# Forward stage of an adaLN transformer kernel: column turns of K, Q and LayerNorm rows moved from TensorE to DMA transposes, and the filler work redistributed over four segments

## The chip, the cores and the metric

One Trainium2 chip, one of its cores. The metric is the device time of one execution in microseconds, as the median of several runs. The profile is that of one execution, with the times of every instruction and DMA issue. Engines: PE is TensorE, PEld its weight loads, DVE is VectorE, ACT is ScalarE, POOL is GpSimd, SP is SyncE. SP does nothing in this kernel but issue DMAs, in program order.

## The reference

The reference runs an adaLN block forward and backward: `_out, _vjp = jax.vjp(_f, ...)`, and returns the output and eleven gradients. What matters here is the forward recurrence, over 64 segments of 32 tokens (model width 512, 32 heads of 128, 8 memory rows, 2048 tokens):

```python
for s in range(n_seg):
    xs = x[:, s * seg_len:(s + 1) * seg_len, :].copy()
    h = jnp.concatenate([mem, xs], axis=1)
    q = jnp.einsum('btd,dhe->bhte', h, Wq)
    k = jnp.einsum('btd,dhe->bhte', h, Wk)
    v = jnp.einsum('btd,dhe->bhte', h, Wv)
    scores = jnp.einsum('bhqe,bhke->bhqk', q, k) * scale
    scores = jnp.where(mask[None, None], scores, -1000000000.0)
    p = _softmax(scores, axis=-1)
    o = jnp.einsum('bhqk,bhke->bhqe', p, v)
    o = jnp.einsum('bhte,hed->btd', o, Wo)
    mem = o[:, :M, :].copy()
    outs.append(o[:, M:, :])
```

Ahead of it stands `h = _layernorm(x) * (1 + ca) + sa`; behind it a second LayerNorm and a gated MLP, and then the whole backward pass. Each segment's first 8 rows (its memory) come from the segment before, so the 64 segments are a chain.

## The kernel before, in words

The kernel is one program in stages. `phase2` is the forward recurrence and the only stage that the change touches; the later stages (MLP forward and backward, the attention's backward recurrence, weight gradients) are the same.

In `phase2` one pass of the loop `for s in range(NS)` handles one segment. Four segments are a **tile** of 128 rows; `s4 = s % 4`. A segment has 40 rows, of which 32 (memory and the first 24 tokens) depend on the chain or are handled with it. The last 8 token rows of each segment, its **tail**, do not depend on memory in their K, Q and V rows. They are therefore computed for a whole tile at once, ahead of time, as PE filler.

Order of one segment on PE: K and Q products of 32 rows (L257), V products (L659), turn of K and Q rows into columns on PE (`turns`, L829), scores (L839), Exp on ACT into `ET` (L841), denominators (L845), P·V (L865), scaling into `Ost` on DVE and ACT (L886, L889), turn of `Ost` into `OT` (`ott`, L857), output product (`outproj`, L223), split into two bfloat16 parts (`split_pair`, L230 and L232), their fold (`sum_pair`, L242), and the copy of the new memory into `hT_next` (L1022), with which the next segment begins. Mask products (`mask_mm`, L783) open the score banks of the next segment.

Into this chain the kernel puts independent work, at named places:

- `fill(s4, "f1")` stands behind the output product, `fill(s4, "f2")` behind the fold, `fill(s4, "turn")` behind the last P·V product. `b_pieces(t)` says what goes there: the tail rows of K and Q of the *next* tile, 8 blocks of 128 columns each (`proj_b`, a call of `col_pass`, L257), written to `RB["k"]` and `RB["q"]`, stored to DRAM by `rows_out` (six DMAs each, L599 and L602) and turned into columns by `turn_b` (L623): eight PE transposes into PSUM, then copies by ACT and DVE into `b_colsk`, `b_colsq`. `tails_in` (POOL, L65) copies each segment's part of these columns into the K and Q operands.
- `p1(j, k)` runs step k of the first LayerNorm of tile j, two tiles ahead: 0 load, 1 statistics, 2 scale, 3 shift, 4 turn (four PE transposes, L420, an ACT copy into `hx`, L422, and a POOL copy of its tail columns into `hb`, L424).
- `TailRows` (object `tail`) does the output product of the four tails of the *previous* tile: 32 accumulating steps (L215), here in pieces of (24, 8) in segment 3, then a split (L314, L315), a fold (L325) and row stores, put into the list `later` and taken from it by `pop_later`.

The order on every engine is that of the program: `self.pin(i0)` ties each instruction to the one before it on its engine. SP's order in one segment is: VT store (L1040), PS store (L1041, of the segment before, after POOL has normalised `Pst`, L1038), K row stores (L594, L595), Q row stores, the transpose of `Vst` into `VTr` (L954), the transpose of `ET` into `Pst` (L962), stores OSR (L997) and OT (L1010), and then, where they fall, the tail row stores (L599, L602), a load of `wmod_r` (L195) and one of x (L394). `Pst`, `VTr`, `ET`, `Ost` and `OT` have one buffer each, so that a later write waits for the DMA that reads it. DMAs of SP use eight semaphores in turn: each waits for the landing of the eighth before it.

Of the kernel before, what the change touches and what calls it, by code (L numbers as in the profile page):

```python
# [9 lines left out]
AF = mybir.ActivationFunctionType  # L10
# [30 lines left out]
class K:  # L41
# [334 lines left out]
    def phase1_setup(self, ctx, psum_tile_fn):  # L376
        nc, tc, cfg, io = self.nc, self.tc, self.cfg, self.io
        D, DC, NT = cfg.D, cfg.DC, cfg.NT
        x_rows = io["A_x"].rearrange("o s d -> (o s) d")
        p1 = ctx.enter_context(tc.tile_pool(name="p1", bufs=1))  # L380
        p1w = ctx.enter_context(tc.tile_pool(name="p1w", bufs=2))
        ca1_bc = self.ca1_bc = p1.tile([128, D], F32, name="ca1_bc")
        sa_bc = self.sa_bc = p1.tile([128, D], F32, name="sa_bc")
        mhalf = p1.tile([128, 1], F32, name="mhalf1")
        nc.gpsimd.memset(mhalf[:], -0.5)
        nseg = 128 // cfg.T

        def p1_tile(j):

            st = {}  # L390

            def load():
                st["x0"] = p1w.tile([128, D], BF16, name="x0_1", bufs=1)
                nc.sync.dma_start(st["x0"][:], x_rows[j * 128:(j + 1) * 128, :])  # L394

            def stats():
                bs = p1w.tile([128, 6], F32, name="st1")
                nc.vector.bn_stats(bs[:], st["x0"][:])
                mv = p1w.tile([128, 2], F32, name="mv1")
                nc.vector.bn_aggr(mv[:], bs[:])  # L400
                ve = p1w.tile([128, 1], F32, name="ve1")
                nc.vector.tensor_scalar_add(ve[:], mv[:, 1:2], EPS)
                rstd = p1w.tile([128, 1], F32, name="rstd1")
                nc.gpsimd.tensor_tensor(rstd[:], ve[:], mhalf[:], op=ALU.pow)
                st.update(mv=mv, rstd=rstd)

            def scale():
                xh = st["xh"] = p1w.tile([128, D], F32, name="xh", bufs=1)
                nc.vector.tensor_scalar(xh[:], st["x0"][:], st["mv"][:, 0:1], st["rstd"][:, 0:1], op0=ALU.subtract, op1=ALU.mult)
                nc.vector.tensor_tensor(xh[:], xh[:], ca1_bc[:], op=ALU.mult)  # L410

            def shift():
                h1 = st["h1"] = p1w.tile([128, D], BF16, name="h1", bufs=1)
                nc.vector.tensor_tensor(h1[:], st["xh"][:], sa_bc[:], op=ALU.add)
                nc.gpsimd.dma_start(self.H1ROWS[j * 128:(j + 1) * 128, :], h1[:])

            def turn():
                tp = psum_tile_fn()
                for c in range(DC):
                    nc.tensor.transpose(tp[:, c, :], st["h1"][:, c * 128:(c + 1) * 128], self.ident[:])  # L420
                hx = p1w.tile([128, DC, 128], BF16, name="hx", bufs=3)
                nc.scalar.activation(hx[:], tp[:, 0:DC, :], AF.Copy)  # L422
                hb = p1w.tile([128, DC, nseg, 8], BF16, name="hb", bufs=2)
                nc.gpsimd.tensor_copy(hb[:], hx[:].rearrange("p c (s t) -> p c s t", t=cfg.T)[:, :, :, 24:cfg.T])  # L424
                return hx, hb

            return load, stats, scale, shift, turn

        return p1_tile

# [8 lines left out]
    def phase2(self):  # L439
        nc, tc, cfg, io = self.nc, self.tc, self.cfg, self.io  # L440
# [14 lines left out]
        with ExitStack() as ctx:  # L455
# [38 lines left out]
            P1_AHEAD = 2  # L494
            NT = cfg.NT
            nseg_t = 128 // T
            hxs = {}

            def p1(j, k=None):
                if j < NT:  # L500
                    if j not in p1s:
                        p1s[j] = p1_tile(j)
                    for i in (range(1, 5) if k is None else [k]):
                        r = p1s[j][i]()
                        if r is not None:
                            hxs[j] = r
# [101 lines left out]
            def b_pieces(t):  # L608

                bt = btails[t] = {}  # L610
                RBt = RB

                def proj_b(x, a, n, eng):
                    hb = hxs[t][1]
                    self.col_pass(psp, Ws[x], 0, lambda c: hb[:, c, :, :].rearrange("p s q -> p (s q)"), RBt[x], eng, steps=(a, n))
                    if a + n == 8:
                        rows_out(RBt[x], DR[x], t * nseg_t, nseg_t)

                def turn_b(x):
                    bt[x] = btp.tile([128, 8, 128], BF16, name="b_cols" + x)  # L620
                    tp = psp.tile([128, 8, 128], BF16, name="turn_ps", tag="p")
                    for i in range(8):
                        nc.tensor.transpose(tp[:, i, :], RBt[x][:, i * 128:(i + 1) * 128], self.ident[:, :])  # L623

                    def f():
                        for hf in range(2):
                            self.evac(("act", "dve")[hf], bt[x][:, 4 * hf:4 * hf + 4, :], tp[:, 4 * hf:4 * hf + 4, :])

                    evacs.append(f)

                P = lambda x, a, n, eng: (lambda: proj_b(x, a, n, eng))
                T_ = lambda x: (lambda: turn_b(x))
                return {(0, "f1"): [P("k", 0, 4, "dve")], (1, "f1"): [P("k", 4, 4, "dve")], (1, "f2"): [P("q", 0, 2, "act")],
                        (2, "turn"): [T_("k")], (2, "f1"): [P("q", 2, 4, "dve")], (2, "f2"): [P("q", 6, 2, "act")],
                        (3, "turn"): [T_("q")]}

            evacs = []

            def evac_turned():
                while evacs:  # L640
# [1 line left out]

            first = b_pieces(0)
            firsts = {x: [first[k][0] for k in ks] + [evac_turned]
                      for x, ks in (("k", ((0, "f1"), (1, "f1"), (2, "turn"))),
                                    ("q", ((1, "f2"), (2, "f1"), (2, "f2"), (3, "turn"))))}
            slots = {}

            VCH = ((0, 4), (4, 4), (8, 3))

# [51 lines left out]
            def fill(s4, where):  # L702
                for f in slots.pop((s4, where), []):
                    f()
# [67 lines left out]
                    nc.gpsimd.dma_start(self.AOA[4 * b + i + 1, 32:32 + M, :].rearrange("r (c x) -> (r c) x", x=128),  # L772
                                        rb[32 * i:32 * i + 32, :])

            tail = TailRows(self, sb2, psp, psp, 1, "ao", rows_b, (24, 8), ptag="p")

            masked = {}

# [24 lines left out]

            for s in range(NS):
                s4 = s % nseg_t
                if s4 == 0:
                    if s > 0:
                        p1(s // nseg_t + P1_AHEAD, 0)
                    slots = b_pieces(s // nseg_t + 1) if s + nseg_t < NS else {}
                hT = get_ht(s)  # L810
                hT_next = get_ht(s + 1) if s + 1 < NS else None
                QT, KT, Vst = XT["q"], XT["k"], Vsts[s % 2]
# [90 lines left out]

                if s < NS - 1 and norms:
                    norms.pop()()
                if s == NS - 1:
                    first_tile[3]()
                proj("k", 0, "dve")
# [21 lines left out]
                    v_tails(0)  # L930
                if s == NS - 1:
                    first_tile[4]()
                v_chunk(s, 0)
                turns()
                v_chunk(s, 1)
# [30 lines left out]
                ost(0, or0, "dve")  # L966
                ost(1, or1, "act")
                den(2, or2)
                if s4 == 3:
                    p1(s // nseg_t + P1_AHEAD, 4)  # L970
                early = s4 == 0 and len(self.later) > 1
                if early:
                    self.pop_later()
                more = list(range(NP)) if s + 1 < NS else []
                if more:
                    mask_mm(more.pop(0))
                pv(2, or2)
                recip(2, 3, or2)
                ost(2, or2, "dve")
                fill(s4, "turn")  # L980
                if s == NS - 1:
                    turn_v(2)
                if more and s4 < 2:
                    mask_mm(more.pop(0))
                ott(0)
                if more:
                    mask_mm(more.pop(0))
                ott(1)
                ott(2)
                if not early:  # L990
                    self.pop_later()
                self.pop_later()
                if s == NS - 1:
# [3 lines left out]
                nc.sync.dma_start(self.OSR[s], gl3(Ost))  # L997
                at_ps = outproj()
                evac_turned()
                if s4 < 3:  # L1000
                    p1(s // nseg_t + P1_AHEAD, s4 + 1)
                if NS - 4 <= s < NS - 1:
                    first_tile[s - NS + 4]()
                elif s == NS - 1:
# [7 lines left out]
                if s == NS - 1:  # L1012
                    first_tile[7]()
                    nc.scalar.activation(self.first_st[:, 11:12], self.first_st[:, 10:11], AF.Sigmoid)
                if s4 == 3:
                    tail.chunk()
                if s == NS - 1:
                    turn_p(0)
# [7 lines left out]
                if s + 1 in mod_at:  # L1026
                    load, products = self.mod_rest(psp, sb2, mod_at.index(s + 1))
                    load()
                    mod_r.append(products)
                if s4 == 3:  # L1030
                    tail.chunk()
                tail.split()
                self.store_rows(psp, sb2, ft, self.AOA[s + 1, 0:32, :], "at", "p")
# [1205 lines left out]
class TailRows:  # L2239
# [45 lines left out]
    def split(self):  # L2285
        if self.whole is None:
            return False
        (ps, s0), self.whole = self.whole, None
        parts = self.k.fold_split(self.pool, ps, self.name + "_b", self.home)

        def summed():
            ft = self.k.fold_sum(self.psp, parts, self.name + "_b", "p")
            to = self.dram_b
            to = (lambda rb: self.dram_b(rb, s0 // 4)) if callable(to) else to[s0 // 4]
            self.k.store_rows(self.psp, self.pool, ft, to, self.name + "_b", "p")

        self.k.later.append(summed)
        return True
# [100 lines left out]
```

## Time and profile before

| | us |
|---|---|
| median of 3 runs | 2996.63 (2991.85 to 3003.91) |
| span of the profiled execution | 2991.0 |
| first products and loads of `phase2` (segment 0) | 18.0 to 60.5 |
| segments 1 to 3 | 60.5 to 102.8 |
| tiles 1 to 14 (segments 4 to 59) | 102.8 to 904.1 |
| last tile (segments 60 to 63) | 904.1 to about 965 |
| PE busy, tiles 1 to 14 | 798.6 of 801.3 |
| mean DMA share, tiles 1 to 14 | 0.88 |

The span is counted from the first to the last instruction of the profiled execution; the runs' times include what lies around it. The profile's page gives busy time per engine, groups of instructions and DMA queues; other views of the trace give busy time in chosen stretches, an engine's instructions in order of time, and all instructions of one line or tile. A DMA issue on SP's queue (SPq) has as its time how long the queue was held by it, not how long the transfer took. The DMA share is the time of all packets over that of 16 engines, so a stretch can show over 1 when its packets end later. Matmul durations overlap; the cost of a group is read from its start to the start of the next.

### The profile page before, as it was taken

What the parts mean: (1) busy time and instruction counts of PE and PEld (TensorE: products, weight loads), DVE (VectorE), ACT (ScalarE), POOL (GpSimd) and SP (SyncE); (2) the same over time, 40 slices, a digit from 0 to 9 for tenths busy, and PEclk for the clock granted to TensorE, in tenths of its full rate; (3) what the DMA queues carried; (4) which work ended last, traced back from release to release, by engine and by line L of the source; (5) the groups of instructions that cost most, each with busy time, mean ns of one, the idle gap of its engine ahead of it and who ended that gap; (6) DMA issues with size and microseconds to landing.
All of it is one profiled execution on the core that took longest, in us unless ns stands there. A gap on an engine that the chain in (4) does not pass through costs nothing.

```text
span 2991.0 us, 105890 instructions
## 1 busy us (share of the span) xinstructions
PE 2932.8 (98%) x43975; PEld 1839.9 (62%) x44049; DVE 1612.4 (54%) x3679; ACT 1271.8 (43%) x3057; POOL 1197.2 (40%) x2456
## 2 busy tenths in 40 slices
PE   6999999999999999999999999999999999999999
PEld 3666666666665544445677777777777754445454
DVE  5566656666655788833456665566566532222230
ACT  2555555555555533312355555555555520011111
POOL 2454555555545222221344444444444422333321
PEclk8999999999999999999999999999999999999999
DMA  9898888889889899998699999999999997766574
GB/s 310 222 223 211 214 217 217 213 214 215 217 218 277 211 230 226 229 290 278 200 251 251 251 253 243 250 250 250 255 255 250 254 281 245 242 207 214 178 245 144
DMA packets 836438, 703.05 MB, mean 235 GB/s; under 512 B 536643, under 2 KB 708851, under 8 KB 835061
## 3 DMA queue, kind: packets, MB, share of 16 engines
q1 hardware_dynamic: 710756, 486.09, 65.5%
q0 software_dynamic: 54640, 148.90, 15.7%
q10 hardware_dynamic: 70560, 61.28, 6.5%
q8 instruction: 347, 5.69, 0.8%
q14 instruction: 135, 1.10, 0.1%
HBM read 294.99 MB, written 276.35 MB: 191 GB/s over the span
## 4 chain that ended last, share of the span: by engine, by line
PE 87%; issue 5%; DMA 3%; DVE 2%; POOL 1%; ACT 1%; SPq 1%; DVEq 0%; POOLq 0%; ACTq 0%
PE pass_ps L257 14%; PE gps L2180 9%; PE dh_ps L215 8%; PE pass_ps L659 5%; PE g_ps L1810 5%; PE gps5o L2195 4%; PE dhq_ps L223 4%; PE at_ps L223 4%; PE mm L1291 3%; PE dh_tps L215 3%; PE gps L1470 3%; PE turn_ps L829 2%; PE mm L1266 2%; PE mm L1251 1%; PE tps L1727 1%
## 5 line engine op out<-in xcount | busy, mean ns | idle before, releaser
L2180 PE MATMUL gps<-rows,hrows 128*128 128x512 bf16 (+2 forms) x2125 | 415.6, 355 | 1.8
L2180 PEld LDWEIGHTS <-hrows 128*128 128x128 bf16 x2160 | 211.3, 98 | 204.5
L61 ACT ACTIVATE ot<-gps 128x512 bf16<-128x512 f32 (+3 forms) x75 | 41.3, 550 | 362.2 <-PE gps L2180 229.1
L1855 POOL COPY dOst<-RAd 96x512 bf16<-96x512 bf16 x128 | 75.3, 613 | 297.8 <-DVE RAd L63 297.8
L1038 POOL TENSOR_TENSOR Pst<-Pst,rden 120x1408 bf16<-120x1408 bf16 x63 | 159.9, 2538 | 77.8 <-issue 49.6
L659 PE MATMUL pass_ps<-Wv,hT 128*32 128x512 bf16 (+2 forms) x2304 | 187.2, 358 | 0.0
L63 DVE CAST ot<-gps 128x512 bf16<-128x512 f32 (+3 forms) x76 | 48.1, 633 | 247.0 <-PE gps L2180 169.9
L2184 POOL DMA_DIRECT2D out_dram<-ot x108 | 81.5, 755 | 249.1 <-DVE ot L63 141.9
L257 PEld LDWEIGHTS <-hT 128*32 128x32 bf16 x4096 | 114.8, 97 | 103.9 <-issue 5.7
L63 DVE CAST Vst<-pass_ps 96x512 bf16<-96x512 f32 x128 | 87.3, 682 | 107.0 <-ACT RBv L61 98.5
L215 PE MATMUL dh_ps<-WvT,dVT 128*32 128x512 bf16 x2048 | 133.3, 380 | 1.7
L659 PE MATMUL pass_ps<-Wv,hb 128*32 128x512 bf16 (+2 forms) x636 | 128.7, 353 | 0.0
L257 PE MATMUL pass_ps<-Wq,hT 128*32 128x512 bf16 x2048 | 123.9, 383 | 4.8 <-DMA Wq<-in_A_Wq_dram 4.8
L257 PE MATMUL pass_ps<-Wk,hT 128*32 128x512 bf16 x2048 | 123.2, 382 | 2.5 <-POOL hT L549 1.1
L223 PE MATMUL at_ps<-Wo,OT 128*32 128x256 bf16 x4096 | 123.9, 273 | 0.7 <-DMA Wo<-in_A_Wo_dram 0.6
L257 PE MATMUL pass_ps<-WoT,dyT 128*32 128x256 bf16 (+1 forms) x3072 | 122.5, 308 | 0.9 <-ACT dyT L1936 0.9
L223 PE MATMUL dhq_ps<-WqT,dQT 128*32 128x256 bf16 x4096 | 122.9, 273 | 0.0
L215 PE MATMUL dh_ps<-WkT,dKT 128*32 128x512 bf16 x2048 | 122.3, 380 | 0.0
L794 POOL DMA_DIRECT2D Vst<-RBv x192 | 99.9, 526 | 55.6 <-ACT ET L841 34.4
L2195 PE MATMUL gps5o<-WoT,rows 128*128 128x512 bf16 x548 | 120.6, 379 | 1.0 <-DMA rows<-OSR 0.4
L223 PEld LDWEIGHTS <-dQT 128*32 128x32 bf16 x4096 | 109.7, 97 | 15.8
L315 DVE TENSOR_TENSOR dST<-dh_ps,dST 128x512 bf16<-128x512 f32 x64 | 44.3, 692 | 129.9 <-ACT dST L314 129.9
(471 smaller groups left out, 6991.2 us busy)
## 6 DMA issues: line engine op xcount, KB each, us to landing
OSR<-Ost SPq DMA_DIRECT2D x64, 352.0 KB
OT<-OT SPq DMA_DIRECT2D x64, 352.0 KB
PS<-Pst SPq DMA_DIRECT2D x64, 352.0 KB
Pst_l<-PS SPq DMA_DIRECT2D x64, 352.0 KB
OT_l<-OT SPq DMA_DIRECT2D x64, 352.0 KB
DVR<-rows_x POOLq DMA_DIRECT2D x64, 352.0 KB, 6.3
DKR<-rows_x POOLq DMA_DIRECT2D x64, 352.0 KB, 5.7
DQR<-rows_x POOLq DMA_DIRECT2D x64, 352.0 KB, 3.4
```

Source lines behind the costliest of these rows:

```text
L63: return nc.vector.tensor_copy(out, in_)
L215: self.nc.tensor.matmul(ps[32 * j:32 * j + 32, :], lhsT=lhsT, rhs=w, start=(n < 4), stop=(n >= total - 4), tile_position=(0, 32 * j))
L223: nc.tensor.matmul(ps[32 * j:32 * j + 32, :], lhsT=x[k], rhs=w[k][:, 256 * d:256 * d + 256], start=(n == 0), stop=(n == total - 1), tile_p ...
L257: self.nc.tensor.matmul(ps[32 * j:32 * j + 32, :], lhsT=lhs(c), rhs=rhs, start=(c == 0), stop=(c == DC - 1), tile_position=(0, 32 * j))
L659: nc.tensor.matmul(ps[32 * j:32 * j + 32, o * E:(o + n) * E], lhsT=lhsT, rhs=wc[:, 3 * a + hl:3 * (a + n - 1) + hl + 1:3, :], start=(c == ...
L794: nc.gpsimd.dma_start(Vst[96 + 8 * j:104 + 8 * j, :], rb[32 * j + o:32 * j + o + 8, :])
L1038: nc.gpsimd.tensor_tensor(Pst[0:120, :, :], Pst[0:120, :, :], rden[:, :].unsqueeze(2).to_broadcast([120, G, 128]), op=ALU.mult)
L1291: nc.tensor.matmul(hp[:], lhsT=xT[:, fc, :], rhs=wT[:, fc, :], start=(n == 0), stop=(n == 2 * FC - 1))
L1470: nc.tensor.matmul(ps[:], lhsT=h2r[:, j, c * 128:(c + 1) * 128], rhs=xr[:, j, :], start=(j == 0), stop=(j == NT - 1))
L1810: nc.tensor.matmul(ps[:, j, 0:w], lhsT=lh[:, g * GW:(g + 1) * GW], rhs=rh[:, g * GW:g * GW + w], start=True, stop=True)
L2180: nc.tensor.matmul(ps[:, 0:ng * E], lhsT=hrows[:, tp_, c * 128:(c + 1) * 128], rhs=rows[:, tp_, 0:ng * E], start=(tp_ == 0), stop=(tp_ == ...
L2195: nc.tensor.matmul(pss[gg][:], lhsT=rows[:, t, gg * E:(gg + 1) * E], rhs=dyrows[:, t, :], start=(n == 0), stop=(n == NTP - 1))
```

## The change

1. For tiles after the first, `turn_b` issues one DMA transpose of `RB[x]` (128x1024) on SP instead of eight PE transposes, an ACT and a DVE copy.
2. From tile 2 on, `p1`'s turn is one DMA transpose of `h1` (128x512) on SP. The POOL copy into `hb` becomes a step of its own (5, `ends`).
3. The pieces of `b_pieces` begin one segment earlier, in segment 3 of the tile two ahead of use, and stand in other places; the turns stand at a new place, `fill(s4, "rows")`, ahead of the V products.
4. `p1`'s steps are one segment earlier, with the load issued at the start of segment 3 (by SP's order right behind the OT store of segment 2).
5. The tail product is cut into (8, 16, 8) and lies in segments 1 and 2 instead of 3; its fold comes in segment 3 instead of 0, and the DVE copy of its rows after the turns of `Ost`.
6. The three mask products stand in the same places in all segments.

```diff
             def turn():
-                tp = psum_tile_fn()
-                for c in range(DC):
-                    nc.tensor.transpose(tp[:, c, :], st["h1"][:, c * 128:(c + 1) * 128], self.ident[:])
                 hx = p1w.tile([128, DC, 128], BF16, name="hx", bufs=3)
-                nc.scalar.activation(hx[:], tp[:, 0:DC, :], AF.Copy)
+                if j < 2:
+                    tp = psum_tile_fn()
+                    for c in range(DC):
+                        nc.tensor.transpose(tp[:, c, :], st["h1"][:, c * 128:(c + 1) * 128], self.ident[:])
+                    nc.scalar.activation(hx[:], tp[:, 0:DC, :], AF.Copy)
+                else:
+                    nc.sync.dma_start(hx[:], st["h1"][:], transpose=True)
                 hb = p1w.tile([128, DC, nseg, 8], BF16, name="hb", bufs=2)
-                nc.gpsimd.tensor_copy(hb[:], hx[:]...)
+                st.update(hx=hx, hb=hb)
+                if j < 2:
+                    ends()
                 return hx, hb
+            def ends():
+                nc.gpsimd.tensor_copy(st["hb"][:], st["hx"][:]...)
...
                 def turn_b(x):
                     bt[x] = btp.tile([128, 8, 128], BF16, name="b_cols" + x)
+                    if t > 0:
+                        nc.sync.dma_start(bt[x][:], RBt[x][:, 0:1024], transpose=True)
+                        return
...
-                return {(0, "f1"): [P("k", 0, 4, "dve")], (1, "f1"): [P("k", 4, 4, "dve")], (1, "f2"): [P("q", 0, 2, "act")],
-                        (2, "turn"): [T_("k")], (2, "f1"): [P("q", 2, 4, "dve")], (2, "f2"): [P("q", 6, 2, "act")],
-                        (3, "turn"): [T_("q")]}
+                pieces = {(3, "f1"): [P("k", 0, 4, "dve")], (3, "f2"): [P("k", 4, 2, "act")], (0, "f1"): [P("q", 0, 4, "dve")],
+                          (0, "f2"): [P("k", 6, 2, "act")], (1, "rows"): [T_("k")], (1, "f1"): [P("q", 4, 4, "dve")],
+                          (2, "rows"): [T_("q")]}
+                if t == 1:
+                    pieces[0, "f1"] = pieces.pop((3, "f1")) + pieces.pop((3, "f2")) + pieces[0, "f1"]
+                return pieces
...
-            slots = {}
+            slots = b_pieces(1)
...
-            tail = TailRows(self, sb2, psp, psp, 1, "ao", rows_b, (24, 8), ptag="p")
+            tail = TailRows(self, sb2, psp, psp, 1, "ao", rows_b, (8, 16, 8), ptag="p")
...
-                if s4 == 0:
-                    if s > 0:
-                        p1(s // nseg_t + P1_AHEAD, 0)
-                    slots = b_pieces(s // nseg_t + 1) if s + nseg_t < NS else {}
+                if s4 == 3:
+                    p1(s // nseg_t + P1_AHEAD + 1, 0)
+                    slots = b_pieces(s // nseg_t + 2) if s + 2 * nseg_t < NS + 3 else {}
...
+                if s4 == 3:
+                    p1(s // nseg_t + P1_AHEAD, 5)
...
+                fill(s4, "rows")
+                if s4 == 2:
+                    p1(s // nseg_t + P1_AHEAD, 4)
                 v_chunk(s, 0)
...
-                if s4 == 3:
-                    p1(s // nseg_t + P1_AHEAD, 4)
-                early = s4 == 0 and len(self.later) > 1
+                early = s4 == 3 and len(self.later) > 1
                 if early:
-                    self.pop_later()
+                    rows_of = self.later.pop(0)(False)
...
-                fill(s4, "turn")
-                if more and s4 < 2:
+                if more:
                     mask_mm(more.pop(0))
...
-                if not early:
+                if early:
+                    rows_of()
+                else:
                     self.pop_later()
...
-                if s4 < 3:
-                    p1(s // nseg_t + P1_AHEAD, s4 + 1)
+                if s4 == 3:
+                    p1(s // nseg_t + P1_AHEAD + 1, 1)
+                elif s4 < 2:
+                    for k in (1, 2) if s == 0 else (s4 + 2,):
+                        p1(s // nseg_t + P1_AHEAD, k)
...
-                if s4 == 3:
+                if s4 == 2:
                     tail.chunk()
...
-                if s4 == 3:
+                if s4 in (1, 2):
                     tail.chunk()
```

## The prediction

> **What bounds the kernel now.** I read the page first, then the busy time of four stretches of the forward stage, then two timelines of the same stretches: TensorE's (PE) and SyncE's queue (SPq). A *segment* is one pass of the loop over `s`; four segments make a *tile* of 128 rows.
>
> ```profile
> PE 2932.8 (98%) x43975; PEld 1839.9 (62%) x44049; DVE 1612.4 (54%) x3679; ACT 1271.8 (43%) x3057; POOL 1197.2 (40%) x2456
> ```
>
> ```profile
> 732.90:747.15 14.25, 14.11 (x281) 9.50 (x278) 9.45 (x24) 8.06 (x21) 6.71 (x13) 1.00 1.05 217
> 747.15:761.17 14.02, 14.02 (x282) 8.99 (x279) 9.00 (x22) 7.73 (x21) 7.91 (x13) 1.00 0.86 202
> 761.17:775.20 14.03, 14.03 (x292) 9.52 (x285) 8.81 (x21) 8.33 (x22) 6.89 (x15) 1.00 0.92 226
> 775.20:790.05 14.85, 14.85 (x304) 10.36 (x297) 7.72 (x19) 8.99 (x24) 8.24 (x21) 1.00 0.86 219
> ```
>
> These are segments 48 to 51 (bounds: the first Wk,hT matmul of each). After the length come PE, PEld, DVE, ACT and POOL busy, then clock, DMA share, GB/s. PE is busy throughout, at full clock; a tile takes 57.15 us, and nearly every tile from segment 12 to 59 repeats these lengths. But the last columns say that the 16 DMA engines are at 0.86 to 1.05. So PE sets the end, and something else is close behind.
>
> A full PE row can still hide waits. PE in segments 49 and 50, from the last PV product to the last transposes of Ost:
>
> ```profile
> 756.18 0.37 PE L783 MATMUL st_ps<-maskT,ident 128*128 128x480 bf16 x1
> 756.52 0.39 PE L857 MATMUL tps<-ident,Ost 120*128 120x120 bf16 x4
> 756.74 0.32 PE L783 MATMUL st_ps<-maskT,ident 128*128 128x360 bf16 x1
> 756.90 0.64 PE L857 MATMUL tps<-ident,Ost 120*128 120x120 bf16 x7
> ...
> 770.20 0.61 PE L623 MATMUL turn_ps<-ident,RBk 128*128 128x128 bf16 x8
> 770.64 0.38 PE L857 MATMUL tps<-ident,Ost 120*128 120x120 bf16 x4
> 770.85 0.37 PE L783 MATMUL st_ps<-maskT,ident 128*128 128x480 bf16 x1
> 771.06 0.53 PE L857 MATMUL tps<-ident,Ost 120*128 120x120 bf16 x7
> ```
>
> Segment 49 needs 1.36 us here (756.18 to 757.54) without a turn, segment 50 needs 1.39 (770.20 to 771.59) with one. The eight transposes, 0.44 us (770.20 to 770.64), lie in a wait for DVE's Ost.
>
> Now SyncE's queue from segment 50 into 51:
>
> ```profile
> 766.22 0.36 SPq L1041 DMA_DIRECT2D PS<-Pst  x1
> 766.68 0.51 SPq L594 DMA_DIRECT2D KST<-RA0k  x1
> 767.25 1.67 SPq L595 DMA_DIRECT2D KST<-RA0k  x1
> 769.02 0.63 SPq L594 DMA_DIRECT2D QST<-RA0q  x1
> 769.70 0.42 SPq L595 DMA_DIRECT2D QST<-RA0q  x1
> 770.38 1.94 SPq L954 DMA_TRANSPOSE VTr<-Vst  x1
> 772.77 1.50 SPq L962 DMA_TRANSPOSE Pst<-ET  x1
> 774.37 0.90 SPq L997 DMA_DIRECT2D OSR<-Ost  x1
> 775.37 0.39 SPq L1010 DMA_DIRECT2D OT<-OT  x1
> 775.86 2.60 SPq L599 DMA_DIRECT2D QST<-RBq  x3
> ```
>
> Each row is one issue and how long the queue was held. There is hardly a gap. And the queue is a closed round: the PS store waits for POOL's norm of Pst (L1038, 2.54 us); the norm waits for the Pst transpose to land (issue 757.60, norm from 763.14: 5.5 us); that transpose is queued behind VTr, and VTr behind the K and Q stores, which stand behind the previous PS store. PS issues at 738.43 and 795.43 bracket a tile: 57.00 us, PE's own period. How much of it is slack shows ahead of VTr, the one place where the queue waits for PE's chain (Vst): idle beyond the 0.23 us that every such step has is 0, 0.42, 0.03 and 0 us in these segments, so the round costs 56.55 us. In segments 28 to 31 the same reckoning gives 57.0 - 1.24 - 1.43 - 0.48 - 0 = 53.8 us. **The queue has 0.6 to 3.3 us of slack per tile.** This decides the case.
>
> **The change, part by part**, per tile.
>
> *PE, removed.* Turn of K (0.44 us), of Q (0.45, 784.61 to 785.06) and of h1 (0.22, L420): 1.11 us; over 15, 15 and 14 tiles 16.5 us (the built program has 296 transposes fewer on PE and 44 more on SP, so the change does what it says). Were all of it on the path, that would be the gain.
>
> *PE, what it was worth.* Segment 2: the turn hid a wait; the mask product goes back to its place in segment 49's pattern, so 14.03 becomes 13.96 (segment 49 without the 0.06 us ao_b transpose, which moves on to segment 0). Segment 1: 13.96. Segment 3: h1's turn (0.22) goes, the tail product shrinks from 24 steps (1.40 us, 787.75 to 789.15) to a four-block pass (0.97, 759.34 to 760.31), and the fold sum (0.20) comes in but lies in the same wait for Ost: 14.85 becomes 14.2. Segment 0: the fold sum leaves and the Ost wait shrinks (the last transposes take 0.88 us in segment 48, 0.64 in 49), -0.27; the ao_b transpose +0.06; the K blocks in the second slot +0.45 beside a mod product that already covered that wait: 14.5. Sum 56.6, **-0.55 us per tile**. Pass columns are the same in number; evacuations removed (ACT 0.60 and DVE 0.42 per turn, ACT 0.6 for hx) were not on the path. Tile 0 takes ten blocks in its first slot instead of four: +1.2 us. The last segment loses its tail product: -1.5.
>
> *SP, added.* Three transposes ahead of VTr: K in segment 1; Q and hx in segment 2. Such transposes are not in this stage, so by the nearest rows: one of 128x512 (L1197, forward MLP) holds the queue 1.20 us, minimum and median; one of 128x1408 (L962) 1.29 to 3.16, median 1.83. hx is the first: 1.2 to 1.3. K and Q (1024 columns) lie between, 1.25 to 1.8; I take 1.5, interpolated by columns. With 0.06 us between issues: 1.5 + 1.5 + 1.25 + 0.2 = **4.4 us per tile**, bounds 3.8 and 5.2. A gain from them is excluded, as they release nothing that the round waits for. The RB stores move a segment earlier and the x load to the end of segment 2: the same issues, no cost; the x load (about 1 us) lies in the norm's wait.
>
> *What is queued behind.* VTr, Pst, OSR and OT, then RB rows, VT, PS. Columns are needed one to two segments later, so their own landing costs nothing. Late is Pst: the next segment's Exp writes ET, which that transpose reads. Exp starts 6.9 us into a segment (768.05 - 761.17) while Pst has landed 2 us into it (norm 763.14); about 4 to 5 us of delay are free, once. After that PE waits.
>
> *The round after.* 53.8 to 56.55, plus 4.4. I take 55.4 (the middle of the two, moved slightly to the fuller, since the queue will be full): **59.8 us per tile**, against PE's 56.6. So the queue sets the period, 2.65 us above today's 57.15.
>
> [...]
>
> **Sum.** Thirteen tiles (2 to 14) at +2.65 = 34.5; tile 0 +1.2; tile 1, still on free slack, -0.55; end -1.5: +33.6, less 0.6 for slack left in tile 2: +33 on the profiled span of 2991.0, so 3024. The runs' median lies 5.6 us above that span; I add it: **3030 us**.
>
> **Rivals.**
> - *The queue keeps pace* (chance 0.30). If the round after stays below PE's 56.6, the gain is PE's: 13 x -0.55 + 1.2 - 0.55 - 1.5 = -8, so 2983 of span and a median of 2988. For it: segments 28 to 31, where 53.8 + 3.8 = 57.6 is within 1 us of PE's period; VTr's hold also varies from 1.28 to 2.7 us, so some of it may be backpressure that the new transposes merely take over. Against: segments 48 to 51. [...]
> - *All removed PE time counts* (0.06): only if Ost's wait did not exist; 16.5 us, 2980. Segments 49 and 50 side by side speak against it.
> - *The slower side* is my forecast (0.64): the round decides once the added issues exceed the slack of 0.6 to 3.3 us. Its own range: 53.8 + 3.8 = 57.6 gives +0.45 x 13, 3001; 56.55 + 5.2 = 61.8 gives +4.6 x 13, 3056.
> - *A held PSUM bank*: the tail product now keeps its bank through all of segment 2. Segment 3 today holds it 1.9 us only; five banks serve passes that free theirs in 1 to 2 us, so I count none. If PE lost one evacuation (0.7 us) per tile: +9 us, inside the range.
>
> **Numbers.** About 0.5% (15 us) is what a measurement of this kernel can tell from no change. Faster by more: 0.06. Within: the rival at 2988 and the lower end of my own case, 0.33. Slower: 0.61. The range takes in the rival's 2988 and goes up to 3052, leaving about 0.1 on each side.
>
> **What would show it.** Right: PE idle ahead of or behind the Exp of segments 3 and 0 that the waits put to the Pst transpose; VTr issued 10 to 14 us into segments 2 and 3 instead of 9 to 10; PS to PS four segments apart near 60 us; PE no longer 98% in slices 2 to 12. K and Q transposes should hold the queue about 1.5 us, hx 1.2. Wrong: VTr back at 8.7 us in segment 0, tiles of 56.6 us. If a transpose of 1024 columns holds the queue well below 1.2 us, or VTr's hold falls by what they take, the forecast falls with it.

## The result, and the profile after

The changed kernel took 3027.82 us (median of 4 runs, 3026.20 to 3032.19), the kernel before 2998.64 beside it: ratio 1.0106, 95% interval 1.0088 to 1.0124. The profiled execution spans 3025.8 us against 2991.0, +34.8. By the first Wk,hT products of the segments, +2.7 of that arise up to segment 3, +29.5 in tiles 1 to 14 (59.34 us each instead of 57.24), +2.5 behind them.

The page's engine line, after:

```profile
PE 2942.4 (97%) x43679; PEld 1850.2 (61%) x43753; DVE 1596.8 (53%) x3649; ACT 1249.2 (41%) x3013; POOL 1191.0 (39%) x2456
```

PE has 296 matmuls fewer and is busy 9.6 us longer. Busy time in the segments of one tile, 16 to 19 (columns as in the prediction: length, five engines, clock, DMA share, GB/s):

```profile
284.54:298.83 14.29, 14.29 (x292) 9.29 (x284) 9.27 (x22) 7.90 (x22) 7.52 (x14) 1.00 0.97 216
298.83:312.94 14.11, 14.11 (x276) 9.94 (x273) 8.02 (x20) 8.04 (x22) 8.54 (x20) 1.00 0.93 212
312.94:328.02 15.08, 14.16 (x272) 8.99 (x269) 7.01 (x17) 7.46 (x20) 6.39 (x13) 1.00 0.93 208
328.02:348.89 20.87, 16.80 (x296) 11.67 (x296) 9.86 (x25) 8.22 (x22) 7.14 (x15) 0.84 0.88 200
```

Two things are new in segment 19: PE stands still for 4.1 us (20.87 - 16.80), and the granted clock is 0.84. Other tiles run clean, that is without such a wait: segments 36 to 39 take 14.29, 14.10, 13.96 and 14.43, together 56.79. The wait, first on ACT, then on PE (in brackets the idle time before the instruction and its releaser):

```profile
339.36 1.39 ACT L854 ACTIVATE ET<-st_ps 128x480 bf16<-128x480 f32 x3 [4.74 <-DMA Pst<-ET]
```

```profile
339.99 0.27 PE L858 MATMUL or_ps<-ones,ET 128*128 128x1 bf16 x4 [3.87 <-ACT ET L854]
```

Exp may not overwrite `ET` until the Pst transpose of segment 18 has read it. SyncE's queue shows why that is late:

```profile
324.88 0.35 SPq L1061 DMA_DIRECT2D PS<-Pst  x1
325.34 0.53 SPq L602 DMA_DIRECT2D KST<-RA0k  x1
325.92 1.06 SPq L603 DMA_DIRECT2D KST<-RA0k  x1
327.09 1.08 SPq L602 DMA_DIRECT2D QST<-RA0q  x1
328.22 0.42 SPq L603 DMA_DIRECT2D QST<-RA0q  x1
328.69 2.23 SPq L630 DMA_TRANSPOSE b_colsq<-RBq  x1
330.96 1.26 SPq L425 DMA_TRANSPOSE hx<-h  x1
332.45 1.27 SPq L972 DMA_TRANSPOSE VTr<-Vst  x1
333.77 1.78 SPq L980 DMA_TRANSPOSE Pst<-ET  x1
```

These issues belong to segment 18 (312.94 to 328.02; the PS store is that of 17), and its Pst transpose goes out 5.75 us into segment 19. The queue has hardly a gap; two new transposes, 3.5 us, stand ahead of VTr. Over the tiles (waits from 102 to 920 us: total, times, longest):

```profile
ACT ET L854 <- DMA Pst<-ET: 29.0, 11, 4.7
PE or_ps L858 <- ACT ET L854: 22.8, 25, 3.9
```

And the clock behind the wait, in stretches of 2 us:

```profile
338.00:340.00 2.00, 0.01 (x1) 0.02 (x2) 0.00 (x0) 0.64 (x2) 0.31 (x1) 0.86 0.71 275
342.00:344.00 2.00, 2.00 (x15) 1.52 (x14) 1.24 (x4) 0.82 (x4) 1.95 (x5) 0.50 0.47 177
348.00:350.00 2.00, 2.00 (x52) 1.33 (x52) 1.25 (x4) 0.58 (x2) 0.17 (x1) 1.00 2.12 155
```

For 6.83 us from 339.4 the clock is 0.50, and the 64 output products, 1.76 us in clean segments, take 2.6. In tiles 1 to 14 this happens six times, 30.7 us in all, and never in the kernel before. An estimate from these figures: 14 x 56.7 (clean tiles), + 22 us of added PE idle (24.9 against 3.0 before), + half of 30.7 for the slow clock = 831; measured 830.8. It comes out a little too well, since some of the slow time lies inside the waits and clean tiles go up to 57.0.

### The profile page after: what moved, and what is told of

Its sections match the earlier page's. It is cut to its first block, busy times and chain, and to the rows that moved or that the text cites. A ratio compares the mean times of both kernels' runs of the same rounds, so it can differ in the third digit from the quotient of the medians.

```text
span 3025.8 us, 105199 instructions
## 1 busy us (share of the span) xinstructions
PE 2942.4 (97%) x43679; PEld 1850.2 (61%) x43753; DVE 1596.8 (53%) x3649; ACT 1249.2 (41%) x3013; POOL 1191.0 (39%) x2456
## 4 chain that ended last, share of the span: by engine, by line
PE 59%; issue 4%; ACT 1%; POOL 1%; DMA 1%; DVE 1%; SPq 0%; POOLq 0%; DVEq 0%; ACTq 0%
PE gps L2200 9%; PE dh_ps L215 8%; PE g_ps L1830 5%; PE pass_ps L257 5%; PE gps5o L2215 4%; PE dhq_ps L223 4%; PE mm L1311 3%; PE dh_tps L215 3%; PE gps L1490 3%; PE mm L1271 2%; PE mm L1286 2%; PE tps L1747 2%; PE mm L1240 1%; PE mm L1244 1%; PE gps L1389 1%
## 5 line engine op out<-in xcount | busy, mean ns | idle before, releaser
L61 ACT ACTIVATE ot<-gps 128x512 bf16<-128x512 f32 (+3 forms) x75 | 41.2, 550 | 363.4 <-PE gps L2200 213.0
L257 PEld LDWEIGHTS <-hT 128*32 128x32 bf16 x4096 | 127.2, 97 | 96.6 <-issue 8.3
L223 PEld LDWEIGHTS <-OT 128*32 128x32 bf16 x4096 | 105.9, 99 | 16.1 <-DVE OT L63 3.4
```

Of the source, the lines that this page charges most:

```text
L223: nc.tensor.matmul(ps[32 * j:32 * j + 32, :], lhsT=x[k], rhs=w[k][:, 256 * d:256 * d + 256], start=(n == 0), stop=(n == total - 1), tile_p ...
L257: self.nc.tensor.matmul(ps[32 * j:32 * j + 32, :], lhsT=lhs(c), rhs=rhs, start=(c == 0), stop=(c == DC - 1), tile_position=(0, 32 * j))
```

## The experiments

Per tile, from the traces (means of tiles 1 to 14). "Hold" is the sum of SP's issue times; "at PS" and "at Pst" the queue's gaps ahead of these two issues; "slack" its gap ahead of VTr beyond 4 x 0.23; PE idle (the sum of its gaps) and "slow", the time at clock 0.50, are totals of the 14 tiles. Ratios are to the kernel before on the same chip. Columns from "tile" on come from the one execution that was profiled; for e2 that was the slowest of six (3016.14 us, the others from 3000.52 on), for e3 the fastest of four (3024.51, the others up to 3038.40).

| kernel | median us | ratio, 95% interval | tile | hold | at PS | at Pst | slack | PE idle | slow |
|---|---|---|---|---|---|---|---|---|---|
| before | 2998.64 | | 57.24 | 44.5 | 6.3 | 0.4 | 1.48 | 3.0 | 0 |
| after | 3027.82 | 1.0106 (1.0088 to 1.0124) | 59.34 | 49.8 | 4.8 | 0.3 | 0.02 | 24.9 | 30.7 |
| e1_turns_on_pe | 3013.98 | 1.0062 (1.0047 to 1.0077) | 58.08 | 43.8 | 5.6 | 0.4 | 3.27 | 6.9 | 0 |
| e2_ps_late | 3006.62 | 1.0037 (1.0022 to 1.0052) | 57.68 | 49.9 | 0.7 | 2.1 | 0.57 | 11.1 | 3.4 |
| e3_et2 | 3033.30 | 1.0122 (1.0103 to 1.0141) | 58.64 | 49.2 | 4.6 | 0.3 | 0.00 | 20.4 | 20.5 |
| e4_hx_on_pe | 3023.61 | 1.0090 (1.0070 to 1.0111) | 58.61 | 48.7 | 5.2 | 0.3 | 0.05 | 18.9 | 3.4 |
| f1_ps_late_qrows | 3020.17 | 1.0068 (1.0054 to 1.0083) | 58.64 | 50.8 | 0.8 | 2.5 | 0.17 | 19.4 | 6.8 |
| f2_before_ps_late | 2999.13 | 1.0005 (0.9996 to 1.0014) | 57.20 | 41.2 | 0.5 | 2.5 | 5.58 | 2.7 | 0 |
| f5_before_dma_turns | 3055.10 | 1.0189 (1.0175 to 1.0204) | 60.73 | 49.1 | 6.6 | 0.4 | 0.06 | 40.0 | 37.5 |
| g1_rows_on_pool | 3038.31 | 1.0129 (1.0116 to 1.0143) | 60.08 | 42.3 | 13.3 | 0.3 | 0.08 | 34.0 | 27.3 |
| g2_rows_pool_ps_late | 3002.94 | 1.0008 (0.9999 to 1.0017) | 56.90 | 43.2 | 3.3 | 1.5 | 2.06 | 3.3 | 0 |
| h1_turns_behind_ot | 3027.27 | 1.0097 (1.0083 to 1.0111) | 58.91 | 51.3 | 2.8 | 0.4 | 0.13 | 24.5 | 6.8 |
| h2_turns_behind_ot_ps_late | 3037.23 | 1.0120 (1.0103 to 1.0137) | 59.39 | 49.5 | 0.4 | 5.0 | 0.25 | 30.5 | 3.4 |

The stages behind the recurrence are the same program in all runs, the ladder g3 below included, yet from segment 63 on they took 2042.6 to 2055.7 us in the profiled executions, so effects are read from the tiles.

**e1: the turns back on PE, everything else as changed.**

```diff
-                if j < 2:
+                if True:
...
-                    if t > 0:
-                        nc.sync.dma_start(bt[x][:], RBt[x][:, 0:1024], transpose=True)
-                        return
...
-                          (0, "f2"): [P("k", 6, 2, "act")], (1, "rows"): [T_("k")], (1, "f1"): [P("q", 4, 4, "dve")],
-                          (2, "rows"): [T_("q")]}
+                          (0, "f2"): [P("k", 6, 2, "act")], (1, "turn"): [T_("k")], (1, "f1"): [P("q", 4, 4, "dve")],
+                          (2, "turn"): [T_("q")]}
...
-                fill(s4, "rows")
-                if s4 == 2:
-                    p1(s // nseg_t + P1_AHEAD, 4)
                 v_chunk(s, 0)
...
+                if s4 == 2:
+                    p1(s // nseg_t + P1_AHEAD, 4)
...
+                fill(s4, "turn")
```

> The changed kernel with all three turns back on TensorE, in the stretch ahead of the Ost transposes, and everything else of the change kept. Queue theory (the three transposes make SyncE's round of 59.5 us per tile longer than PE's 56.7): the round falls back to 54 to 57 us, Exp does not wait for the Pst transpose, tiles of about 57.2 us, time 2990 to 3003. Rival, the new places of the filler passes and the tail product (with its PSUM bank held through a segment) cost the time: it stays at 3020 to 3030.

Hold 43.8, slack 3.27, no Exp wait for the Pst transpose, no slow clock: the transposes are what fills the queue. The round, tile less slack, is 58.08 - 3.27 = 54.8 us here, against 57.24 - 1.48 = 55.8 in the kernel before. Segments 38 and 39:

```profile
601.16:616.21 15.05, 14.71 (x284) 9.84 (x281) 7.62 (x18) 8.44 (x22) 7.81 (x20) 1.00 0.95 220
616.21:630.53 14.32, 14.26 (x296) 10.06 (x296) 9.59 (x25) 8.23 (x22) 7.05 (x15) 1.00 0.76 191
```

Segments 0 and 3 take 14.29 and 14.32, as in the changed kernel's clean tiles. Both time ranges missed (measured 3014, between them), for a reason outside the theories: segment 2 takes 15.05 instead of 13.96. Q's and h1's turns now both fall there, and by the timeline h1's ACT copy (0.61 us) goes ahead of the evacuation of OT, with 0.31 us of PE wait ahead of the output product. So in the tiles no cost of spreading the filler shows, but PE turns at these places cost 1.4 us a tile over a clean one.

**e2: the PS store behind the next segment's K and Q row stores.**

```diff
-                if s < NS - 1 and norms:
-                    norms.pop()()
+                put_ps = norms.pop()() if s < NS - 1 and norms else None
...
                 proj("q", 1, "act")
+                if put_ps:
+                    put_ps()
```

> The changed kernel with only the PS store issued later: behind the K and Q row stores of the next segment and not ahead of them, so that the queue does not stand still while POOL normalises Pst. All transposes stay, bytes and packets are the same. Queue theory (a round closed by the norm): the stores no longer stand in the round, Exp stops waiting, tiles of 56.6 to 56.9 us, time 2986 to 2996, below the kernel before. Rival, the DMA engines themselves are full (share 0.99): nothing changes, 3018 to 3030.

Same issues, another order: the wait at PS falls from 4.8 to 0.7 us, the tile by 1.66. The gain was not all that the theory expected (57.68, not 56.9 at most; 3006.62 us, not below the kernel before), and the rival of no change missed too. Over tiles 1 to 14 the DMA share of the changed kernel was 0.92, and 0.79 to 1.13 in single segments. Many tiles are clean (segments 20 to 27: 56.7 each), the rest wait in segment 3. Part of the gain comes back as a new wait: the Pst transpose overwrites `Pst` and must let the late PS store land first (the queue's own waits):

```profile
SPq L981 <- DMA PS<-Pst: 24.4, 23, 1.8
```

**e3: two `ET` buffers** (space from other buffers: `hx` has two instead of three).

```diff
-            ET = ptiles("ET", 1)[0]
+            ETs = ptiles("ET", 2)
```

> The changed kernel with two ET buffers, so that Exp need not wait for the Pst transpose of the segment before (to make room, hx has two buffers and the scaled rows of the first LayerNorm use the scratch of the first MLP tile). Queue theory: the round of about 59.5 us per tile is as long as before, so PE is stopped a little later by the next single buffer, Ost (read by the OSR store) or OT, and the time stays at 3012 to 3028. Rival, the single ET buffer is the cause: 2986 to 2996.

The Exp wait is gone and another stands in its place, on the next buffer that the queue reads late:

```profile
DVE Ost L902 <- DMA OSR<-Ost: 21.6, 10, 3.9
ACT Ost L899 <- DMA OSR<-Ost: 21.1, 10, 3.9
```

The slack ahead of VTr is 0.00: the queue is the limit, and `ET` only where it first showed. The median, 3033.30 us, lies above the expected range; as the profiled execution was the fastest, its tiles do not show why.

**e4: h1's turn back on PE, K and Q by DMA.**

```diff
-                if j < 2:
+                if True:
...
-                if s4 == 2:
-                    p1(s // nseg_t + P1_AHEAD, 4)
                 v_chunk(s, 0)
...
+                if s4 == 2:
+                    p1(s // nseg_t + P1_AHEAD, 4)
```

> The changed kernel with the LayerNorm turn (hx) back on TensorE, in the stretch ahead of the last PV product in segment 2; K and Q stay DMA transposes. Queue theory by hold time (hx holds the queue 1.27 us of 4.5 added): the round falls by 1.3 to 1.5 us per tile, time 3006 to 3014. Rival, the cost goes by columns moved (512 of 2560): 3020 to 3024. If only redistribution counts: 3026 to 3032.

Hold falls by 1.1 only, the wait at PS rises by 0.3, segment 2 takes 14.53 us at the median instead of 13.96 (waits included), the slack stays near nothing. One transpose fewer is not enough; the expectation was too good. The time, 3023.61, lies in the range of the rival by columns moved, and nothing here tests that rival further.

**f1: e2, with Q's tail row stores moved to segment 2.**

```diff
-                    if a + n == 8:
+                    if a + n == 8 and (x == "k" or t == 0):
...
+                if t > 0:
+                    pieces[2, "f1"] = [lambda: rows_out(RBt["q"], DR["q"], t * nseg_t, nseg_t)]
```

> The kernel of e2 with the six row stores of Q's tail moved, for tiles 1 to 15, from the end of segment 1 to behind the OT store of segment 2; no issue is added or left out. Theory that the queue's order and length set the waits (it holds 49.9 us in a tile of 56.6, so it need not be the limit if no stretch of it is late): no Exp waits for the Pst transpose, tiles of 56.7 to 56.9 us, 2986 to 2996 us. Rival, that the total of the queue's holds and landings keeps it behind wherever its issues stand: tiles as in e2, 57.5 to 58, 3002 to 3010 us.

Worse than e2, and slower than both expectations. VTr's holds grew from 8.8 to 9.8 us a tile, the wait at Pst from 2.1 to 2.5, and the Exp waits, small now, fall in segments 2, 3 and 0. Here the issues moved out of one full segment filled another.

**f2: the kernel before with e2's edit alone.**

> The kernel before with only the PS store issued later, behind the next segment's K and Q row stores. Theory that PE sets the pace of the kernel before and its queue has slack: no change, tiles of 57.1 to 57.25 us, 2992 to 3002 us. Rival, that the queue holds the kernel before too (the slack ahead of VTr was nearly 0 in segments 49 to 51): faster, tiles of 56.7 or less, 2980 to 2990 us.

The slack rises from 1.48 to 5.58 us a tile and the time stays: the kernel before is bound by PE, as the prediction read it, and the late store is worth something only where the queue is full.

**f5: the kernel before with the three DMA turns at the old places.**

```diff
+                if j >= 2:
+                    hx = p1w.tile([128, DC, 128], BF16, name="hx", bufs=3)
+                    nc.sync.dma_start(hx[:], st["h1"][:], transpose=True)
...
+                    if t > 0:
+                        nc.sync.dma_start(bt[x][:], RBt[x][:, 0:1024], transpose=True)
+                        return
```

> The kernel before with only the three turns made DMA transposes at their old places (K and Q behind the last PV product of segments 2 and 3, hx in segment 3); filler, steps and stores stay where they were. The old places leave K's and Q's columns less time to arrive. Theory that the added 4.4 to 4.6 us of queue per tile are the cost, not the redistribution: waits of Exp for the Pst transpose as in the changed kernel, tiles of 58.5 to 60 us, 3015 to 3045 us. Rival, that the new places (three transposes ahead of VTr in segments 1 and 2, spread filler) are the cost: tiles of 57.2 or less, 2985 to 3002 us.

Slower than expected, by another mechanism: the tail columns of h1 are used at once, and POOL's copy into `hb` waits for the transpose, then PE for POOL, in segment 0.

```profile
POOL hb L422 <- DMA hx<-h: 145.0, 14, 11.8
PE pass_ps L668 <- POOL hb L422: 31.4, 13, 4.5
```

It does show what issuing the turns a segment or two ahead of use is good for, but not which of the two theories holds: Exp does not wait for the Pst transpose, and the POOL waits may hand the queue the time that it lacks.

**g1: the twelve tail row stores of a tile on POOL's queue.**

```diff
-                    nc.sync.dma_start(dram[s0:s0 + 4, 96 + 8 * j:...
+                    nc.gpsimd.dma_start(dram[s0:s0 + 4, 96 + 8 * j:...
```

> The changed kernel with the twelve tail row stores of each tile issued from POOL's queue instead of SP's; the same bytes in the same places. They held SP's queue 7.5 us per tile (3.78 + 3.68), and POOL's issues elsewhere in the stage take 0.53 us each, so POOL gets 6.4 us per tile more. Theory that the length of SP's round is the cause: hold 49.8 - 7.5 = 42 us per tile, hardly a wait of Exp for the Pst transpose, tiles of 56.7 to 57.0 us, 2988 to 2996 us. Rival, that the load of the DMA engines is the cause, whatever queue issues (mean share near 0.9): the transposes land as late as now, tiles of 58.5 to 59.5 us, 3015 to 3030 us. Against both: POOL's copies of the K and Q tail columns, now behind six issues, come late for the scores; then PE waits for kT or qT in segments 0 and 1.

Slower than the changed kernel, though SP holds 7.5 us a tile less: the queue now waits 13.3 us at PS instead of 4.8. These row stores stand between the Pst transpose and the PS store, beside the transfer and POOL's norm; taken away, they leave a wait there. And the norm itself comes later: it starts 6.4 and 6.9 us after the Pst transposes of segments 0 and 1, against 5.6 and 5.1 in the changed kernel, 2.6 us more a tile over all four segments. In segment 0 part of this is POOL itself, which is still issuing when the transpose has landed; in 8 of 14 tiles the norm starts there without idle time before it:

```profile
718.96 1.82 POOL L607 DMA_DIRECT2D KST<-RBk  x3
720.77 1.75 POOL L610 DMA_DIRECT2D KST<-RBk  x3
...
723.25 2.54 POOL L1058 TENSOR_TENSOR Pst<-Pst,rden 120x1408 bf16<-120x1408 bf16 x1
```

The theory that the length of holds alone decides fell here, and so did the rival's range; the waits for kT or qT that spoke against both did not come. That the closed round decides fits, but g1 does not show it cleanly, since it also made the norm later.

**g2: g1 and e2 together.**

> The kernel of g1 with the PS store issued behind the next segment's K and Q row stores, as in e2. Queue theory: no waits at all, tiles of 56.7 to 56.8 us, 2986 to 2994 us, which is all that the change can bring. Rival (DMA engines): tiles of 57.5 us or more, 3002 us or more.

The same tile as above, segments 18 and 19:

```profile
305.03:318.99 13.96, 13.96 (x272) 8.91 (x269) 7.01 (x17) 7.46 (x20) 10.34 (x20) 1.00 0.86 233
318.99:333.31 14.32, 14.26 (x296) 10.11 (x296) 9.60 (x25) 8.23 (x22) 6.98 (x15) 1.00 1.16 236
```

No wait of Exp for the Pst transpose, full clock, 56.67 us for the tile, with the same bytes and a DMA share up to 1.16; in all fourteen tiles such a wait comes once (1.8 us on ACT). So it is the queue and not the DMA engines, by the tiles. The median time, 3002.94 us, missed the theory's range and lies at the rival's edge, since what was gained in the tiles was lost outside them. Four kernels stand in a square: as changed 59.34, shorter 60.08, PS late 57.68, both 56.90.

It is also the best form of the change that the runs found, and no faster than the kernel before. Fourteen tiles gain 4.7 us; the start loses 3.1; behind segment 60 the profiled execution is 7.8 us longer. Whether that last part belongs to this kernel or to the spread named above stays open.

**h1: the three transposes behind the OT store, and h2: h1 with the PS store late.**

```diff
-                fill(s4, "rows")
-                if s4 == 2:
-                    p1(s // nseg_t + P1_AHEAD, 4)
                 v_chunk(s, 0)
...
                 nc.sync.dma_start(self.OT[s], gl3(OT))
+                fill(s4, "rows")
+                if s4 == 2:
+                    p1(s // nseg_t + P1_AHEAD, 4)
```

> The changed kernel with its three DMA transposes issued behind the OT store of the same segments instead of ahead of VTr; PE's order is the same, no issue is added or left out. Ring theory: what counts of the queue is only what is issued between a PS store and the next Pst transpose (19.8 us of holds per tile in the kernel before, 25.6 in the changed one, 24.7 with the row stores on POOL); what is issued between Pst and the next PS store lies beside Pst's landing and POOL's norm (some 8 us). The turns then leave the ring: its tight length falls to about 55.5 us, below PE's 56.7; tiles of 56.7 to 57.2 us, 2988 to 3000 us. Rival, that the total length of SP's queue counts (49.8 us of holds plus its gaps): tiles as in the changed kernel, 59 us or more, 3020 to 3030 us. Third, that segment 1 with Q's row stores overflows the 8 us: tiles of 57.5 to 58.5 us, 3002 to 3014 us.

> The kernel of h1 with the PS store issued behind the next segment's K and Q row stores, as in e2 (which took the row stores out of the ring there). Ring theory: two cuts of the ring, no waits at all, tiles of 56.7 to 56.8 us, 2986 to 2996 us. Rival (total length of the queue): tiles of 57.7 us as in e2, 3003 to 3010 us.

Both ring expectations missed. The rival by total length came close in h1 (58.91 us and 3027.27 us, where it said 59 or more and 3020 to 3030) but not in h2 (59.39 instead of 57.7), so neither model of the queue carries both runs. In h1, SP from the Pst transpose of segment 33 to its PS store:

```profile
548.67 3.15 SPq L977 DMA_TRANSPOSE Pst<-ET  x1
...
553.31 1.62 SPq L630 DMA_TRANSPOSE b_colsk<-RBk  x1
555.02 2.08 SPq L607 DMA_DIRECT2D QST<-RBq  x3
557.14 1.83 SPq L610 DMA_DIRECT2D QST<-RBq  x3
559.02 0.45 SPq L1060 DMA_DIRECT2D VT<-VTr  x1
559.59 0.37 SPq L1061 DMA_DIRECT2D PS<-Pst  x1
```

That stretch takes 10.4 us on average, where landing and norm take 7.5 in the changed kernel: the third expectation, an overflow in segment 1, named the place, though not the size. The changed kernel waits ahead of the PS stores of segments 2 and 3 only (2.3 and 2.1 us), so K's turn found no room in segment 1. The wait at PS fell by 2.0 us a tile, but the same issues held the queue 1.5 us longer, and little was left. In h2 the wait at Pst takes over:

```profile
SPq L978 <- DMA PS<-Pst: 65.3, 54, 2.6
```

**g3: the price of a wait by itself**, in the kernel before, with no DMA in it.

```diff
+                    for _ in range(1 + (s // nseg_t if pi == 0 and s4 == 1 and 4 <= s < 60 else 0)):
                         nc.scalar.activation(... AF.Exp, scale=cfg.scale)
```

> The kernel before with the first Exp piece of segment 1 of tile t repeated t times more (t = 1 to 14, the same values written again, about 0.47 us each), so that PE waits for ACT by a length that grows from tile to tile and no DMA has a part in it. Theory that a wait of PE costs more than itself, by a halved granted clock afterwards: from some length on segment 1 grows by the wait plus about 2 us, the clock at 0.5 for 3.4 or 6.8 us behind the wait; by the changed kernel's trace the length lies between 1.3 and 1.6 us, so from t = 4 or 5 on. Rival, that the slow clock came from something else in the changed kernel (the burst of transposes): segment 1 grows by the wait alone, the clock at 1.00 throughout. Sum of the repeats 49 us, less what ACT has free ahead of each: 3030 to 3070 us.

One run, 3072.15 us. PE's waits, with their lengths in brackets (segments 9, 13, 29 and 33, so 2, 3, 7 and 8 repeats), and the lengths and clocks of these segments:

```profile
184.33 0.25 PE L846 MATMUL or_ps<-ones,ET 128*128 128x1 bf16 x4 [0.79 <-ACT ET L842]
...
243.22 0.25 PE L846 MATMUL or_ps<-ones,ET 128*128 128x1 bf16 x4 [1.40 <-ACT ET L842]
...
490.21 0.26 PE L846 MATMUL or_ps<-ones,ET 128*128 128x1 bf16 x4 [3.81 <-ACT ET L842]
...
553.17 0.27 PE L846 MATMUL or_ps<-ones,ET 128*128 128x1 bf16 x4 [4.41 <-ACT ET L842]
```

```profile
175.62:190.78 15.16, 14.16 (x280) 9.04 (x278) 8.96 (x22) 8.87 (x23) 7.82 (x13) 1.00 0.67 182
233.91:250.99 17.08, 15.48 (x282) 9.90 (x278) 9.15 (x22) 9.44 (x24) 8.14 (x15) 0.90 0.81 200
478.49:497.62 19.13, 15.13 (x280) 9.89 (x278) 9.14 (x22) 11.73 (x28) 7.77 (x13) 0.91 0.65 169
540.84:561.45 20.61, 16.01 (x283) 10.36 (x279) 9.16 (x22) 12.30 (x29) 8.25 (x15) 0.83 0.66 167
```

Against 14.01 without a repeat, a wait of 0.79 costs 1.15 us (0.21 of it a second small wait), one of 1.40 costs 3.07, of 3.81 5.12, of 4.41 6.60. The rival fell: behind a wait without a DMA the clock went to 0.50 all the same. In this ladder it began at 1.40 us, by the third repeat, since each repeat delays PE by 0.60 us and not the 0.47 that I had taken.

## Why the prediction was right, point by point

- **PE, -0.55 us a tile**: right. Clean tiles take 56.7 to 57.0, some 0.5 us less than before, where 1.11 us of turns were taken off PE.
- **SP, +4.4 us**: right. Per tile K holds 1.49 us (median of one 1.32), Q 1.84 (1.69), hx 1.27 (1.27), together 4.6 without gaps. All holds rose by 5.3 (44.5 to 49.8), as those of other issues grew by 0.7, VTr's among them. These are holds, as are those of the kernel before (medians for 352 KB: 0.39 us as OT, 1.83 as Pst); how long the transfers took stands in no row.
- **The round, 59.8 us**: right in size. PS to PS takes 59.5 us, the slack ahead of VTr is 0.02, and tiles take 59.34. The rival that the queue keeps pace fell with it. The "middle of the two" for the round before, 55.4, had no better ground than that; it fitted, as the mean slack of all fourteen tiles gives 55.8. One term was missing: the moved row stores, counted as "no cost", fill the wait ahead of the PS store of segment 0 (4.1 us before, 0.2 after) and open one of 2.3 us at that of segment 2, so the waits at PS fall by 1.5 us a tile. 55.8 + 5.3 - 1.5 = 59.6 is what the round was made of (59.5 measured); that 55.4 + 4.4 comes so near is partly luck.
- **Where it shows**: half right. PE's waits at Exp lie almost all in segment 3, none over 0.3 us in segment 0; the Pst transposes of segments 0 to 3 go out 12.7, 15.2, 18.5 and 16.8 us after their segment's start, with 4.4 to 5.6 us until the norm can start, and only the third lands after the time of the next Exp (6.9 us into the next segment). VTr goes out 16.7 and 14.9 us into segments 2 and 3, later than the 10 to 14 expected. It is not a steady 2.65 us each tile either: waits of 1.2 to 3.9 us come in eight of the fourteen tiles.
- **"After that PE waits"**: this step lacked a term. Behind six of these eight waits the clock also fell to 0.50, which by the estimate above made up 15.4 of the 37 us above clean tiles. The queue uses that time to catch up, hence clean tiles behind a stalled one: in tile 4 PE takes 64.4 us and the round 62.0, in tile 9 56.8 and 58.6. The forecast fitted since the queue's period sets the mean, however it is paid; besides the waits at PS, no gap of the queue in these tiles is longer than 0.45 us.
- **Ends**: mis-sized. Up to segment 3 2.7 us were lost, not 1.2; the end lost 2.5 instead of gaining 1.5, as segments 61 and 62 waited too (14.60 and 17.51 us against 14.01 and 13.96). The tiles lost 29.5 us where the sum had 33.4 (34.5 - 0.55 - 0.6), so the errors nearly cancel, which is luck.
- **A held PSUM bank**: no such wait appears among the kernel's waits.

What stays argued, not shown: why holds grow when waits go (h1, f1), so that a full queue yields less than its issues suggest. That the three transposes fill the queue is shown by e1 and g2; a rule that says beforehand what a given order of issues will cost is not, as e2, f1, h1 and h2 all missed.

## What to carry to other kernels

Before moving work from a full engine to a DMA queue, add up that queue's holds and gaps over one period and find the wait that closes its round; here 1.5 us of slack stood against 4.6 us of new issues. In these runs a queue that waited at one place was not idle there for use elsewhere: removing issues beside such a wait gave nothing (g1: 7.5 us less of holds a tile, 8.5 us more of wait at PS, where the norm also came later), and moving the wait alone gave part (e2: 1.66 us a tile). Taking work off the engine that bounds a kernel gained only what had not lain in its waits: 1.11 us of turns less on PE made a clean tile some 0.5 us shorter.

## What the runs showed of the hardware

- TensorE's granted clock fell to 0.50 after waits of 1.40 us and more in the ladder (g3) and 1.43 and more in the changed kernel, for 3.41 us, 6.83 or 10.24 (waits of 7.4 and 8.0 us, g3); waits up to 1.33 us left it at 1.00 in these two. Over all runs the lengths with and without it overlap: in the fourteen traces (segments 1 to 61) none of 131 waits of 0.4 to 1.1 us was followed by the slow clock, 19 of 44 between 1.1 and 2.6 were (1.10 us in f1 was, 2.52 in f5 was not), and all 26 longer ones. The slow stretches of one trace begin whole multiples of 3.41 us apart, in the tiles of the changed kernel at 216.54, 339.42, 516.91, 694.41, 755.85 and 871.90 us. With each trace cut into such lengths of 3.41 us, each of the 45 slow stretches begins right behind one in which PE stood still for 1.32 us or more in all (1.49 to 3.30 for these six); of some 3500 other lengths only four held more than 1.4 us of standstill (1.59 to 1.85) without it, in the changed kernel none more than 1.33. There the wait of 3.70 us from 751.27 put 1.16 us into one length and 2.54 into the next, and the clock fell behind the second, at 755.85.
- In the changed kernel the shortest hold of a DMA transpose was 1.26 us for 128x512 (`hx`), 1.27 for 128x1024 (K and Q) and 1.39 for 128x1408 (Pst): 0.13 us more for 2.75 times the columns. The medians were 1.27, 1.32 (K), 1.69 (Q) and 1.92, and single holds of the same issue reached 2.5 us (K) and 2.7 us (Q).
